# Score pairs three ahead and one behind the projection products in the last sections of a fused Fourier-mixing and attention kernel

## The chip, the cores and the metric

The kernel runs on one core of a Trainium2 chip. The metric is the device time of one execution in microseconds (us), lower is better; the median of the runs shown is taken.

## The reference

Two branches of the same input x (2048 tokens of 512 numbers) are mixed by a gate:

```python
g = _sigmoid((x * gate_w).sum(-1, keepdims=True))
# a: Fourier mixing, real part only
a1 = einsum("bsd,ed->bse", x, dft_hid_re);  b1 = einsum("bsd,ed->bse", x, dft_hid_im)
a  = einsum("ts,bse->bte", dft_seq_re, a1) - einsum("ts,bse->bte", dft_seq_im, b1)
# b: softmax attention, 32 heads of 16, scale 16 ** -0.5
q, k, v = split_heads(x @ wqkv)
b  = merge_heads(softmax(q @ k.T * scale) @ v) @ wo
return g * a + (1 - g) * b
```

(The names are shortened; wqkv and wo are scaled so that the scores are large.)

## The kernel before

**Attention in units.** The 32 heads are taken as 16 pairs. The scores of a pair are computed transposed: 128 keys on the partitions, 512 queries along the row. A unit is one pair, 128 keys and 1024 queries, which makes 512 units (`UNITS`). A unit needs four score tiles of 128x512, one for each of two heads and two blocks of queries. `scores` (L782) issues the matmul of one such tile (L795, PE) and its exponential (L796, ACT), which goes from PSUM to the SBUF tile `pt`. The operands of a score matmul lie on 64 partitions: head 0 on partitions 0 to 63, head 1 on 64 to 127. The matmuls of the two heads therefore run side by side in the two halves of the array, and the two together are called a pair of score matmuls here. `values`, through `pv` (L843) and for the last 16 units through `pv_last` (L803), multiplies the exponentials with the values and accumulates in the bank `acc`; four narrow products run side by side, so that the 16 matmuls of two calls show as one group.

**PSUM.** There are eight banks. Bank 6 is `acc`, one bank belongs to the pool `psD` (tiles named d), and the other six form two rings of three: `psS` (tiles named s) and `psA` (tiles named a). `Ring.tile` (L51) takes the bank of its ring that was used longest ago, where a use is the allocation of a tile or, by `finish` (L659), the reading of a finished product. A matmul that takes a bank waits until the last reader of the tile before has ended.

**The last sections.** Most of the kernel is a stream of short patterns in which Fourier products and projection products alternate with scores. The change is behind them, in the loop over `u` from 492 to 510 in steps of two (L1044): ten sections of two units each. A section issues four pairs of score matmuls (`i` = 0 to 3; head 0 goes to an s bank, head 1 to an a bank, from the list `three`), then two calls of `values`, which take the two units of the section before. Between the pairs stand the section's whole projection products: matmuls over all 128 partitions (L469), listed in `whole` as (generator, number of matmuls). A generator yields chains of nine or three matmuls into one bank, and behind the last matmul of a chain `finish` puts the result on DVE (L668). The first chain of a section goes to an s bank in section 492, to the bank d in 494 to 506, and to an a bank in 508 and 510; in 496, 498, 500 and 504 a second chain goes to an s bank. The chains of 508 are a, d, s, and those of 510 are a, d, s, a. In section 506 `turn` (L728) and in 508 `back` (L739) of the object `LastPair` are issued behind the products: `turn` sums and transposes the first half of the last head pair's output into an s bank, from which DVE makes `on` (L734, L736); `back` transposes `on` into an a bank, which ACT and DVE read (L102, L103). Just ahead of section 492 stand four single score matmuls of head 1, in the banks s, s, a, d (L1034).

Each engine works through its own queue in the written order: the schedule is written by hand (`manual_schedule`), and nothing reorders it.

Of the kernel before, what the change touches and what calls it, by code (L numbers as in the profile page):

```python
# [31 lines left out]
def mix_kernel(ctx: ExitStack, tc: tile.TileContext, xa_t, xa, wqkv, w_hid, w_seq, wo, gate_w, out):  # L32
# [749 lines left out]
    def scores(u, qb, h, bank=(psS, "s"), number=None):  # L782
        p, r = divmod(u, 32)
        hf, kt = divmod(r, 16)
        q0 = hf * 1024 + qb * 512
        if u >= UNITS - 16:

            blk, kt = divmod(kt, 8)
            q0, kt = 1024 + blk * 512, 2 * kt + qb
        if u not in pts:  # L790
            pts[u] = work.tile([P, 4, 512], F32, name="pt", bufs=4)
        pool, name = bank
        ps = pool.tile([P, 512], F32, name=name) if number is None else pool.tile([P, 512], F32, name, number)
        rr = slice(64 * h, 64 * h + (64 if p else 50))
        nc.tensor.matmul(ps, ks[p % 2][rr, kt * P:(kt + 1) * P], qs[p % 2][rr, q0:q0 + 512], start=True, stop=True)  # L795
        return nc.scalar.activation(pts[u][:, 2 * qb + h], ps, AF.Exp, bias=0.0, scale=DH ** -0.5)  # L796
# [74 lines left out]
    def pump(gen, n):  # L871
        for x in take(gen, n, False):
            issue(x, None)
# [35 lines left out]
    def run_plan(u):  # L909
        for v in sorted(v for v in plan if v <= u + 1):  # L910
            for f in plan.pop(v):
                f()
# [32 lines left out]
    def values(close=False):  # L945
        nonlocal valued
        i = pv(valued, close)
        valued += 1
        return i
# [94 lines left out]
    for u in range(valued + 2, UNITS, 2):  # L1044
        run_plan(u)
        for i in range(4):
            if i == 2:
                for gen, n in whole[u]:
                    pump(gen, n)
                if u == 506:  # L1050
                    last_pairs[0].turn()
                elif u == 508:
                    last_pairs[0].back()
            for h in range(2):
                scores(u + i // 2, i % 2, h, three[h])
        values()
        values()
# [40 lines left out]
```

## Time and profile before

| what | value |
|---|---|
| time, median of 3 runs | 1666.66 us (1665.65 to 1666.8) |
| profiled execution, its own time | 1666.87 us |
| its span in the profile | 1665.0 us |
| PE (TensorE matmul), busy | 1655.8 us, 13040 matmuls |
| DVE, busy | 1380.5 us |
| ACT, busy | 1266.4 us |
| granted TensorE clock, mean | 0.999 |
| ten last sections (first score pair of 492 to the products behind 510) | from about 1601 to 1651.78 us in the span |

In rows of the timeline the first number is the start in us from the beginning of the span and the second is the length in us; then come the engine, the line, the operation, the tiles it writes and reads, its shape and how often it stands there. A bracket at the end is the idle time of the engine ahead of the row, and what ended it. The lengths of matmuls overlap, because they are pipelined: what a group costs is read from its start to the start of the next group.

### The profile page before, as it was taken

Reading aid. Unit: us, or ns where it says so; the run is one execution under the profiler, and the core shown is the slowest. Engines: PE = TensorE matmul, PEld = TensorE weight load, DVE = VectorE, ACT = ScalarE, POOL = GpSimd, SP = SyncE. Lnnn points to the kernel's source line nnn. Section 1 sums busy time; section 2 is a strip of 40 time slices with the busy share of each in tenths; the row PEclk is TensorE's granted clock in tenths of the full one; section 3 lists DMA queues with packets and bytes.
Section 4 is the critical chain, followed back from the end, with each engine's and each line's share of the span. In section 5 each row is a group of like instructions: output and inputs, shape, how many; then the busy total and the mean of one; then the engine's idle time right before and its main releaser. Section 6 shows DMA issues by size and latency. Waiting matters only on the chain.

```text
span 1665.0 us, 34810 instructions
## 1 busy us (share of the span) xinstructions
PE 1655.8 (99%) x13040; PEld 1008.9 (61%) x13040; DVE 1380.5 (83%) x2361; ACT 1266.4 (76%) x2469; POOL 720.2 (43%) x734
## 2 busy tenths in 40 slices
PE   9999999999999999999999999999999999999998
PEld 7888855556556655666566655665566656644443
DVE  5439888888888888888888888888888888899954
ACT  5312388888888888888888888888788878889996
POOL 0202144454444456544444465554445556433430
PEclk9999999999999999999999999999999999999999
DMA  8973610414151342414157434315141535462114
GB/s 289 349 163 111 185 17 8 70 34 85 40 96 47 70 110 81 97 46 78 46 88 254 88 118 94 88 57 91 51 86 58 111 104 118 141 188 40 34 34 140
DMA packets 82690, 166.71 MB, mean 100 GB/s; under 512 B 19664, under 2 KB 20158, under 8 KB 78510
## 3 DMA queue, kind: packets, MB, share of 16 engines
q1 hardware_dynamic: 78282, 163.53, 39.1%
q8 instruction: 103, 1.69, 0.5%
q0 software_dynamic: 3808, 0.30, 0.2%
q14 instruction: 65, 0.53, 0.1%
q10 hardware_dynamic: 432, 0.66, 0.1%
HBM read 109.14 MB, written 54.65 MB: 98 GB/s over the span
## 4 chain that ended last, share of the span: by engine, by line
PE 98%; DMA 1%; DVE 0%; issue 0%; POOL 0%; ACT 0%; SPq 0%; DVEq 0%; POOLq 0%; ACTq 0%
PE acc L843 28%; PE d L469 24%; PE a L291 18%; PE s L795 16%; PE s L383 3%; PE s L415 1%; PE d L383 1%; PE a L108 1%; PE a L106 1%; PE s L108 1%; PE s L106 1%; PE a L107 1%; PE s L107 1%; PE a L469 1%; PE s L469 0%; DMA raw<-xa_t 0%
## 5 line engine op out<-in xcount | busy, mean ns | idle before, releaser
L293 DVE TENSOR_REDUCE mx<-a 128x1 f32<-128x512 f32 x2026 | 1259.5, 683 | 170.9 <-PE a L291 144.6
L796 ACT ACTIVATE pt<-s 128x512 f32<-128x512 f32 x2006 | 1022.0, 621 | 33.7 <-PE s L795 17.8
L291 PE MATMUL a<-ks,qs 64*128 64x512 f32 (+1 forms) x2026 | 723.8, 407 | 0.0
L795 PE MATMUL s<-qs,ks 64*128 64x512 f32 (+1 forms) x2006 | 664.2, 395 | 0.8 <-DVE on L736 0.6
L469 PE MATMUL d<-xab,ch 64*128 64x512 f32 x2016 | 644.8, 394 | 0.0
L823 POOL TENSOR_TENSOR oe<-oe,part 128x512 f32<-128x512 f32 x215 | 278.4, 1295 | 597.4 <-ACT part L822 594.9
L291 PEld LDWEIGHTS a<-ks,qs 64*128 64x128 f32 (+1 forms) x2026 | 361.2, 184 | 213.7 <-issue 118.2
L843 PE MATMUL acc<-pt,vt 128*17 128x512 f32 (+1 forms) x3968 | 487.2, 599 | 0.0
L795 PEld LDWEIGHTS s<-qs,ks 64*128 64x128 f32 (+1 forms) x2006 | 361.4, 184 | 71.3 <-ACT pt L796 27.3
L469 PE MATMUL d<-xab,cl 64*128 64x512 f32 x1008 | 397.9, 395 | 0.0
L469 PEld LDWEIGHTS d<-xab,ch 64*128 64x128 f32 x2016 | 366.7, 184 | 27.1
L822 ACT COPY part<-acc 128x512 f32<-128x512 f32 x215 | 126.3, 588 | 187.5 <-PE acc L843 186.5
L843 PEld LDWEIGHTS acc<-pt,vt 128*17 128x17 f32 (+1 forms) x3968 | 92.9, 102 | 218.6 <-issue 138.9
L469 PEld LDWEIGHTS d<-xab,cl 64*128 64x128 f32 x1008 | 185.6, 184 | 13.6
L454 POOL TENSOR_TENSOR cl<-craw,ch 128x512 fp32r<-128x512 f32 x126 | 162.4, 1289 | 10.1
L469 PE MATMUL d<-wre,xab 64*128 64x512 f32 x336 | 90.4, 402 | 0.0
L469 PEld LDWEIGHTS d<-wre,xab 64*128 64x128 f32 x336 | 59.9, 184 | 40.3 <-issue 12.1
L453 POOL CAST ch<-craw 128x512 fp32r<-128x512 f32 x126 | 77.1, 612 | 16.2 <-PE s L795 13.6
L323 POOL DMA_DIRECT2D qs<-mt x119 | 67.2, 570 | 9.9 <-PE a L291 4.9
L469 PE MATMUL d<-wo_hl,o_hl 64*128 64x512 f32 (+1 forms) x246 | 65.2, 397 | 0.0
L102 ACT CAST hl<-s 128x512 fp32r<-128x512 f32 x28 | 16.2, 588 | 58.9 <-PE s L383 31.3
L469 PEld LDWEIGHTS d<-wo_hl,o_hl 64*128 64x128 f32 (+1 forms) x246 | 44.2, 185 | 16.4 <-ACT pt L796 10.2
(172 smaller groups left out, 1034.0 us busy)
## 6 DMA issues: line engine op xcount, KB each, us to landing
craw<-w_seq SPq DMA_DIRECT2D x128, 256.0 KB
qk<-hl SPq DMA_DIRECT2D x32, 512.0 KB
qs<-qk SPq DMA_DIRECT2D x96, 128.0 KB
ks<-qk SPq DMA_DIRECT2D x96, 128.0 KB
b<-hl SPq DMA_DIRECT2D x16, 512.0 KB
xab<-b SPq DMA_DIRECT2D x16, 512.0 KB
o<-oe SPq DMA_DIRECT2D x62, 128.0 KB
oh<-nh SPq DMA_DIRECT2D x12, 512.0 KB
```

The lines of the kernel that those rows point to most:

```text
L291: nc.tensor.matmul(ps, qs[p % 2][r, qt * P:(qt + 1) * P], ks[p % 2][r, kb * 512:(kb + 1) * 512], start=True, stop=True)
L293: user = nc.vector.tensor_reduce(mx[p % 2][:, h, qt, kb:kb + 1], ps, AX.X, ALU.max)
L323: (nc.gpsimd if own else nc.sync).dma_start(rows.rearrange("v (q b c) -> v b q c", q=8, b=4)[:, b], mt[hf][32 * b + h:32 * b + 32:2])
L383: i = nc.tensor.matmul(ps, st[r], mv[r], start=not half and not j, stop=half == 1 and j == 11)
L453: nc.gpsimd.tensor_copy(h1, raw)
L454: nc.gpsimd.tensor_tensor(l1, raw, h1.bitcast(F32), ALU.subtract)
L469: i = nc.tensor.matmul(self.ps, st[r], mv[r], start=not self.begun, stop=stop)
L795: nc.tensor.matmul(ps, ks[p % 2][rr, kt * P:(kt + 1) * P], qs[p % 2][rr, q0:q0 + 512], start=True, stop=True)
L796: return nc.scalar.activation(pts[u][:, 2 * qb + h], ps, AF.Exp, bias=0.0, scale=DH ** -0.5)
L822: nc.scalar.copy(part[0], acc)
L823: nc.gpsimd.tensor_tensor(total, total, part[0], ALU.add)
L843: i = nc.tensor.matmul(acc[32 * j:32 * j + width], v[:, 16 * h:16 * h + width], pt[:, j], start=begin, stop=done or close)
```

## The change

In the ten sections the place at which the projection products (and `turn` or `back`) are issued moves from behind the second pair of score matmuls to behind the third. The exponentials move with their pairs, so that on ACT the cast of `back` (L102) comes behind six exponentials of section 508 instead of four. The number of instructions on each engine is the same, and the orders on DVE, POOL and SP are unchanged. As the rings hand out banks in the order of use, the chains and pairs of these sections also land on other banks.

```diff
@@ -1044,7 +1044,7 @@
     for u in range(valued + 2, UNITS, 2):
         run_plan(u)
         for i in range(4):
-            if i == 2:
+            if i == 3:
                 for gen, n in whole[u]:
                     pump(gen, n)
                 if u == 506:
```

## The prediction

> **What bounds the kernel now.** I read the page first, then the timeline of PE over the last sections, and beside it that of ACT.
>
> ```profile
> PE 1655.8 (99%) x13040; PEld 1008.9 (61%) x13040; DVE 1380.5 (83%) x2361; ACT 1266.4 (76%) x2469; POOL 720.2 (43%) x734
> PE 98%; DMA 1%; DVE 0%; issue 0%; POOL 0%; ACT 0%; SPq 0%; DVEq 0%; POOLq 0%; ACTq 0%
> ```
>
> The first line is the busy time of the engines, the second the chain that ended last, by engine. PE is busy for 99% of the span and makes 98% of the chain. An edit to PE's order therefore pays only through time that PE loses or stops losing. Section 494 shows what an undisturbed section costs on PE:
>
> ```profile
> 1606.43 0.49 PE L795 MATMUL s<-qs,ks 64*128 64x512 f32 x1
> ...
> 1606.77 0.39 PE L795 MATMUL s<-qs,ks 64*128 64x512 f32 x1
> ...
> 1607.09 1.67 PE L469 MATMUL d<-wo_hl,o_hl 128*128 128x512 f32 x6
> 1608.69 0.50 PE L795 MATMUL s<-qs,ks 64*128 64x512 f32 x1
> ...
> 1609.03 0.39 PE L795 MATMUL s<-qs,ks 64*128 64x512 f32 x1
> ...
> 1609.36 1.91 PE L843 MATMUL acc<-pt,vt 128*17 128x512 f32 x16
> 1611.20 0.50 PE L795 MATMUL s<-qs,ks 64*128 64x512 f32 x1
> ```
>
> From start to start: the two leading pairs take 0.34 and 0.32 us, the six products 1.60 (so a chain of three takes 0.80), the two pairs behind 0.34 and 0.33, and the values 1.84. Nothing idles. The same stretch on ACT, whose exponentials free the score banks:
>
> ```profile
> 1607.02 0.60 ACT L796 ACTIVATE pt<-s 128x512 f32<-128x512 f32 x1 [0.51 <-PE a L795]
> 1607.52 0.59 ACT L796 ACTIVATE pt<-a 128x512 f32<-128x512 f32 x1
> 1607.99 0.60 ACT L796 ACTIVATE pt<-s 128x512 f32<-128x512 f32 x1
> 1608.47 0.62 ACT L796 ACTIVATE pt<-a 128x512 f32<-128x512 f32 x1
> ```
>
> ACT starts 0.59 us behind the first pair, so the s bank of that pair is free 1607.62 - 1606.43 = 1.19 us and its a bank 1608.11 - 1606.43 = 1.68 us behind the pair's start. The next exponentials follow in steps of (1608.47 - 1607.02) / 3 = 0.48. These delays are what the change runs into.
>
> **Part 1: the pairs themselves.** Four pairs stay four pairs, but 2 + 2 becomes 3 + 1. What three in a row cost is shown by three rounds of another row-tiled product behind the last section:
>
> ```profile
> 1651.78 0.49 PE L751 MATMUL s<-w,o 32*128 32x512 f32 x1
> ...
> 1652.12 0.39 PE L751 MATMUL s<-w,o 32*128 32x512 f32 x1
> ...
> 1652.35 0.39 PE L751 MATMUL s<-w,o 32*128 32x512 f32 x1
> ...
> 1652.68 1.91 PE L803 MATMUL acc<-pt,vt 128*17 128x512 f32 x16
> ```
>
> The first costs 0.34, the middle one 0.23, the last 0.33: a round is 0.23, and entering or leaving the row tiling adds about 0.10 each. So three pairs cost 0.90. No row shows a lone pair. If it pays both ends, it costs 0.23 + 0.20 = 0.43; if the ends overlap, no less than 0.33, the price of a pair with one end. From above the nearest row is a single full product, 0.55 us to the next group, part of which is a wait for ACT:
>
> ```profile
> 1654.53 0.50 PE L469 MATMUL s<-wo_hl,o_hl 128*128 128x512 f32 x1
> 1655.08 1.10 PE L732 MATMUL s<-pairsum,oe 128*128 128x64 f32 x8
> ```
>
> I take 0.43, since both ends are in the rows above. Then 0.90 + 0.43 = 1.33 stands against 1.34 before: nothing, ten times. The ends give -0.10 or +0.12 per section, so -1.0 to +1.2 us over ten. [...]
>
> **Part 2: sections whose products open in the bank d (494 to 506).** The third pair takes the third bank of each ring, so the next s chain must use the first pair's s bank again. It starts 0.90 + 0.80 = 1.70 us behind that pair and needs 1.19: no wait. If this cover went (ACT late by over 0.5 us), each 0.1 us beyond would cost 0.1 us in 496, 498, 500 and 504. The fourth pair starts 1.7 us or more behind the first and lands on the first or second pair's banks. Of these the latest is the second pair's s bank, by ACT's 0.48 steps free at about 1.19 + 0.96 = 2.15, wanted at 0.90 + 1.60 = 2.50 where an s chain stands; where none does, the banks are the first pair's, free at 1.19 and 1.68, wanted from 1.70 on: just enough. ACT is no bound: eight exponentials are 8 x 0.48 = 3.8 us in a section of 4.77 (1606.43 to 1611.20), and in a section with three products, shorter by 0.8, still 4.0. The values use exponentials of the section before, which end earlier than now. Cost 0.
>
> **Part 3: section 492.** Its products open in the s ring, behind four extra scores, where ACT is in arrears. First PE, then ACT:
>
> ```profile
> 1601.13 0.50 PE L795 MATMUL s<-qs,ks 64*128 64x512 f32 x1
> ...
> 1601.62 2.35 PE L469 MATMUL s<-wo_hl,o_hl 128*128 128x512 f32 x9
> ...
> 1604.25 0.39 PE L795 MATMUL s<-qs,ks 64*128 64x512 f32 x1
> ...
> 1604.58 1.92 PE L843 MATMUL acc<-pt,vt 128*32 128x512 f32 x16
> ```
>
> ```profile
> 1600.45 1.12 ACT L796 ACTIVATE pt<-s 128x512 f32<-128x512 f32 x2
> 1601.42 0.64 ACT L796 ACTIVATE pt<-a 128x512 f32<-128x512 f32 x1
> ...
> 1602.37 0.67 ACT L796 ACTIVATE pt<-s 128x512 f32<-128x512 f32 x1
> ```
>
> The four extra scores are exponentials one to four; the row at 1602.37 is the first pair's s tile. Now the products use the bank of the second extra score, freed at 1600.45 + 1.12 = 1601.57, and start at 1601.62, so a release takes 0.05. In the changed order the third pair takes that bank, its a tile the bank of the third extra score (1602.06), and the products get the first pair's s bank: 1602.37 + 0.67 + 0.05 = 1603.09. They start 1.47 us later; behind them stands one pair of 0.43 instead of two (1604.58 less 1604.25 is 0.33 for the second, the first 0.34). Net 1.47 - 0.24 = +1.23 us.
>
> **Part 4: section 510.** Its products open in the a ring:
>
> ```profile
> 1645.67 0.49 PE L795 MATMUL s<-qs,ks 64*128 64x512 f32 x1
> ...
> 1646.33 0.97 PE L469 MATMUL a<-wo_hl,o_l 128*128 128x512 f32 x3
> ...
> 1649.28 0.49 PE L795 MATMUL s<-qs,ks 64*128 64x512 f32 x1
> ...
> 1649.94 1.91 PE L803 MATMUL acc<-pt,vt 128*17 128x512 f32 x16
> ```
>
> ```profile
> 1646.75 0.59 ACT L796 ACTIVATE pt<-a 128x512 f32<-128x512 f32 x1
> ```
>
> Now the third a bank is free and the products start at once. In the changed order they need the first pair's a bank: 1646.75 + 0.59 + 0.05 = 1647.39, 1.06 us later than 1646.33. Behind them 0.43 instead of 0.66: net +0.83 us. Then follow the values, the end products and the last pair in one PE queue, with no wait on ACT that was late; the loss reaches the end.
>
> **Part 5: sections 502 and 508, where PE waits now.**
>
> ```profile
> 1625.71 0.50 PE L795 MATMUL s<-qs,ks 64*128 64x512 f32 x1 [0.17 <-DVE yp L668]
> ```
>
> ```profile
> 1637.61 1.91 PE L803 MATMUL acc<-pt,vt 128*17 128x512 f32 x16
> 1640.12 0.47 PE L795 MATMUL s<-qs,ks 64*128 64x512 f32 x1 [0.59 <-DVE on L736]
> ...
> 1640.78 0.96 PE L469 MATMUL a<-wo_hl,o_l 128*128 128x512 f32 x3
> ```
>
> Both first pairs wait for an s bank that DVE still reads: the last s chain of 500, and `turn` of 506. In the changed order the first pair finds a free bank and the second waits, 0.34 later. In 502 that is enough: about -0.2. In 508 the first pair starts at 1637.61 + 1.84 - 0.2 = 1639.25, the second still at 1640.12, and the products, which open in the first pair's a bank, not before 1639.25 + 1.68 + 0.05 = 1640.98. That is 0.20 later than 1640.78, less 0.23 for the pair that no longer stands behind: about 0 for both sections together, the 0.2 being inside it. `back` takes the second pair's a bank, free long before its turn. Its cast waits on ACT behind two more exponentials, with two exponentials instead of four queued behind it; ACT idles there, and only the end products need the cast, eight us on.
>
> [...]
>
> **The sum.** 1.23 + 0.83 + 0 + 0 = +2.06 us. The profiled execution took 1666.87 us for a span of 1665.0, 1.87 outside it, and lies 0.2 above the median of 1666.66. I add 2.1 to the median: **1668.8 us**, +0.13%.
>
> **The rivals.**
>
> *Forecast: bank waits in 492 and 510 alone, about +2.1.* Chance 0.62. With part 1's own bounds +1.1 to +3.3.
>
> *The ends of a lone pair overlap (0.33).* For it: PE starts a group before the last one's modelled end (values at 1609.36, pair ends 1609.42). Against it: every first and last pair pays. It gives -1.0, a little less since in 508 DVE sets the second pair's start: about +1.2, 1667.9 us. Chance 0.15.
>
> *The lone pair drains twice, slower by over 0.2%.* Place: the ten single pairs between products and values. Each enters 64-row tiling and leaves it before the array is full; if the next group waits for the pair's whole end, 0.50 us (1608.69), plus the entry's 0.10, it costs 0.60, 0.17 more than taken, 1.7 in all: +3.8, 1670.5 us. It decides from 0.55 us on, which the single full product reaches but with ACT's wait in it. [...] The rows agree with 0.10 per end in groups of two and more. Chance 0.17.
>
> *The waits are hidden and the change gains.* If PE's early start lets ACT run ahead, so that 492 and 510 lose nothing, what is left is -0.2 in 502, about -0.3 in 508 and up to -1.0 from overlapping ends: -1.5, 1665.2 us. Against it: ACT cannot start before the pair it reads, and 1.68 exceeds 0.90. Chance 0.06. That the change does not do what it says is excluded: the built order on PE has three pairs ahead in all ten sections.
>
> **How the numbers follow.** About 0.2% (3.3 us) is what a measurement of this kernel can tell from no change; the runs shown spread over 1.15 us. Forecast, overlap and gain all end within it: same 0.62 + 0.15 + 0.06, less 0.01 for a gain beyond 0.2% and 0.02 for the forecast's upper end, is 0.80; slower 0.17 + 0.02 = 0.19; faster 0.01. The range runs from the overlap case less half the runs' spread, 1667.3, to the drained pair's 1670.5; what is left out is the gain and the tail above.
>
> **What would show it.** In the profile after: in 492 the nine products start about 1.5 us behind the third pair's s matmul, released by ACT `pt` L796; in 510 the first a chain starts about 1.7 us behind the first pair; 502's wait is gone, in 508 the wait for `on` stands ahead of the second pair; lone pairs at 0.43 us; sections 494 to 500 as long as now to 0.1 us. It is wrong if PE waits in 494 to 506, if the lone pair lies outside 0.33 to 0.55, or if the tail behind 510 changes its length.

## The result

| | before | changed |
|---|---|---|
| time, median of 15 runs | 1666.66 us (1665.3 to 1667.2) | 1669.26 us (1668.42 to 1671.2) |
| profiled execution, its own time | 1666.87 us | 1671.2 us |
| its span | 1665.0 us | 1669.1 us |

The ratio of the times is 1.0018 (95% interval 1.0011 to 1.0024): the change makes the kernel slower by 1.8 to 4.0 us, 2.6 us by the medians. The forecast was 1668.8 us in a range of 1667.3 to 1670.5. The profiled execution of the changed kernel is the slowest of its 15 runs, for a reason that the profile shows.

First the page of the changed kernel, its busy times:

```profile
PE 1660.0 (99%) x13040; PEld 1011.5 (61%) x13040; DVE 1379.8 (83%) x2361; ACT 1265.7 (76%) x2469; POOL 718.8 (43%) x734
```

The work of the other engines is the same to 1.5 us, and PE is busy for 4.2 us more with the same 13040 matmuls. Of this 1.0 us lies in the first 100 us, far ahead of the change (98.50 against 97.51 us busy), and 2.3 us in section 492, where single matmuls fill the time and, as shown below, the products take longer. The list of waits of PE between 1600 and 1656 us (who waits for whom, us in total, times, longest) shows the waits, the first two lines for before, the last two for the changed kernel:

```profile
PE s L795 <- DVE on L736: 0.6, 1, 0.6
PE s L795 <- DVE yp L668: 0.2, 1, 0.2
```

```profile
PE a L469 <- ACT pt L796: 1.2, 2, 0.8
PE s L469 <- ACT pt L796: 0.5, 1, 0.5
```

Both old waits, for DVE, are off the list, and three waits for ACT stand there, all at the opening of a product group: 492 (s), 508 and 510 (a). The wait for `on` has only become too short for the list: the second pair of 508 starts 0.52 us behind the first (1642.64 and 1643.16) instead of 0.34. The timeline of PE in section 492 of the changed kernel, from the last extra score on:

```profile
1601.30 0.39 PE L795 MATMUL d<-qs,ks 64*128 64x512 f32 x1
...
1602.19 0.50 PE L795 MATMUL s<-qs,ks 64*128 64x512 f32 x1
1602.68 0.50 PE L795 MATMUL a<-qs,ks 64*128 64x512 f32 x1
1603.66 3.91 PE L469 MATMUL s<-wo_hl,o_hl 128*128 128x512 f32 x9 [0.48 <-ACT pt L796]
1607.51 0.49 PE L795 MATMUL s<-qs,ks 64*128 64x512 f32 x1
...
1607.94 1.93 PE L843 MATMUL acc<-pt,vt 128*32 128x512 f32 x16
```

The third pair and the nine products start where the banks come free. The bank of the products is freed by the exponential of the first pair's s tile, which ends at 1603.60:

```profile
1602.93 0.67 ACT L796 ACTIVATE pt<-s 128x512 f32<-128x512 f32 x1
```

But the products then take 1607.51 - 1603.66 = 3.85 us, where 2.29 was their price before. The table by stretches says why. Behind each stretch stand its length, the busy time of PE, PEld, DVE, ACT and POOL, the granted clock of TensorE, and last the share and the rate of the DMA:

```profile
1602.00:1603.00 1.00, 1.00 (x4) 0.37 (x2) 0.00 (x0) 1.00 (x4) 0.92 (x3) 1.00 0.23 66
1603.00:1604.00 1.00, 0.52 (x2) 0.30 (x2) 0.21 (x1) 1.00 (x4) 0.86 (x2) 0.96 0.00 0
1604.00:1605.00 1.00, 1.00 (x4) 0.76 (x3) 0.00 (x0) 1.00 (x4) 1.00 (x1) 0.50 0.03 10
...
1606.00:1607.00 1.00, 1.00 (x3) 0.75 (x3) 0.00 (x0) 0.06 (x1) 0.00 (x0) 0.50 0.03 4
1607.00:1608.00 1.00, 1.00 (x8) 0.25 (x10) 0.39 (x1) 0.00 (x0) 0.00 (x0) 0.83 0.01 2
```

The granted clock falls to 0.50 just behind the start of the products and is back at 1 in 1607.3. A mean of 0.96 means half clock for 0.08 of the first microsecond, 0.83 for 0.34 of the last; with the three full ones between that makes one spell of 3.42 us. What stands ahead of it, from about 1601.7 to 1603.66, is called the thin stretch below: PE runs score matmuls there mostly one by one, each when ACT frees its bank, and then waits for 0.48 us.

Section 510, and the pairs around it, in the changed kernel:

```profile
1647.12 1.91 PE L803 MATMUL acc<-pt,vt 128*17 128x512 f32 x16
1648.96 0.50 PE L795 MATMUL s<-qs,ks 64*128 64x512 f32 x1
...
1649.31 0.40 PE L795 MATMUL s<-qs,ks 64*128 64x512 f32 x1
...
1649.55 0.39 PE L795 MATMUL s<-qs,ks 64*128 64x512 f32 x1
...
1650.70 0.96 PE L469 MATMUL a<-wo_hl,o_l 128*128 128x512 f32 x3 [0.76 <-ACT pt L796]
...
1653.64 0.50 PE L795 MATMUL s<-qs,ks 64*128 64x512 f32 x1
...
1654.07 1.91 PE L803 MATMUL acc<-pt,vt 128*17 128x512 f32 x16
```

The products start 1.74 us behind the first pair, when the exponential of its a tile has ended at 1650.65:

```profile
1650.06 0.59 ACT L796 ACTIVATE pt<-a 128x512 f32<-128x512 f32 x1
```

The lone pair behind them takes 1654.07 - 1653.64 = 0.43 us.

From one landmark to the next, the two profiled executions compare so:

| stretch | before | changed | difference |
|---|---|---|---|
| start to the last extra score (d) | 1600.72 | 1601.30 | +0.58 |
| from there to the values of 492 | 3.86 | 6.64 | +2.78 |
| to the values of 508 | 39.25 | 39.18 | -0.07 |
| to the values of 510 | 6.11 | 6.95 | +0.84 |
| to the end of the span | 15.06 | 15.03 | -0.03 |

The first row lies ahead of the change, where both programs have the same order: it is the spread from one execution to the next. Of the second row 1.56 us are the half clock; the other 1.22 are the later start of the products, less what one pair behind them saves.

### The profile page after: what moved, and what is told of

It is laid out like the page before. It is cut to its first block, busy times and chain, and to the rows that moved or that the text cites. A ratio compares the mean times of both kernels' runs of the same rounds, so it can differ in the third digit from the quotient of the medians.

```text
span 1669.1 us, 34802 instructions
## 1 busy us (share of the span) xinstructions
PE 1660.0 (99%) x13040; PEld 1011.5 (61%) x13040; DVE 1379.8 (83%) x2361; ACT 1265.7 (76%) x2469; POOL 718.8 (43%) x734
## 4 chain that ended last, share of the span: by engine, by line
PE 99%; DMA 0%; ACT 0%; issue 0%; DVE 0%; DVEq 0%; SPq 0%; ACTq 0%
PE acc L843 28%; PE d L469 25%; PE a L291 17%; PE s L795 16%; PE s L383 3%; PE s L415 1%; PE d L383 1%; PE a L108 1%; PE a L106 1%; PE s L108 1%; PE s L106 1%; PE a L107 1%; PE s L107 1%; PE acc L803 1%; PE s L469 1%; PE a L469 1%
## 5 line engine op out<-in xcount | busy, mean ns | idle before, releaser
L102 ACT CAST hl<-s 128x512 fp32r<-128x512 f32 x28 | 16.1, 587 | 58.9 <-PE d L383 16.5
```

## The experiments

Times are medians; the kernel before on the same chip had 1666.54 us beside the first four experiments, 1666.58 beside the four from "The bank without the move" on, and 1666.26 beside the last one and the repeat of the eight sections. Sections are compared in the traces between the same landmarks as above, since no median of one section's edit is clear of its interval.

**Section 492 alone.**

```diff
-            if i == 2:
+            if i == (3 if u == 492 else 2):
```

> Only section 492 has three pairs ahead; the other nine keep two and two. Theory A (bank wait, and behind it sometimes a spell at half clock): the nine products start 1.47 us later than before, when ACT has freed the first pair's s bank; net +1.23 us from the section's first pair to its values at full clock, and up to +2.8 us where the clock falls as in the profile after. Median +1.2 to +2.8. Theory B (the wait alone, the half clock of the one profile was chance): +1.2, no granted clock under 1 in this section. Theory C (the loss comes from the ten lone pairs): about +0.1.

Measured 1667.72 us, ratio 1.0007 (0.9998 to 1.0016): by itself not clear of no change. The trace:

```profile
1600.26 0.39 PE L795 MATMUL d<-qs,ks 64*128 64x512 f32 x1
...
1602.63 2.32 PE L469 MATMUL s<-wo_hl,o_hl 128*128 128x512 f32 x9 [0.49 <-ACT pt L796]
1604.88 0.50 PE L795 MATMUL s<-qs,ks 64*128 64x512 f32 x1
...
1605.32 1.92 PE L843 MATMUL acc<-pt,vt 128*32 128x512 f32 x16
```

The same wait, but the products take 2.25 us: the clock held, at 1.00 in every microsecond from 1600 to 1608. From the last extra score (d) to the values it is 5.06 us, +1.20 against the 3.86 of before. So the wait costs 1.2 us in both traces, and the half clock comes on top in some executions only.

**The changed kernel once more**, unedited.

> The changed kernel once more, unedited, for a second trace of section 492. Theory A: the product start in 492 is again released by ACT 2.6 us behind the first pair; the nine products take either about 2.3 us (clock held) or up to 3.9 us (half clock), and the runs spread over about 1.6 us more than those of the kernel before. Theory B: the products take 2.3 us and the runs lie as close together as before.

Measured 1668.93 us, ratio 1.0016 (1.0007 to 1.0025). Its trace has the same d, and products that start at the same time as in the experiment above:

```profile
1600.27 0.39 PE L795 MATMUL d<-qs,ks 64*128 64x512 f32 x1
...
1602.63 3.90 PE L469 MATMUL s<-wo_hl,o_hl 128*128 128x512 f32 x9 [0.49 <-ACT pt L796]
1606.47 0.50 PE L795 MATMUL s<-qs,ks 64*128 64x512 f32 x1
```

```profile
1602.00:1603.00 1.00, 0.51 (x2) 0.37 (x2) 0.21 (x1) 1.00 (x4) 0.59 (x1) 0.82 0.00 0
...
1606.00:1607.00 1.00, 1.00 (x8) 0.40 (x11) 0.42 (x1) 0.00 (x0) 0.00 (x0) 0.98 0.01 2
```

Up to the products the two executions agree to 0.01 us, and one falls to half clock and the other does not. Nothing in the order of PE up to there tells them apart. The spell lasts 0.36 + 3 + 0.04 = 3.40 us. The mean granted clock of a whole run shows the spell too, though coarsely. It is rounded to 0.001, which is what a spell costs (half of 3.4 us in 1669), and in the traces before and after the change the clock also falls at the end of the kernel (at 1662.78 and 1665.37 us), behind the last matmul. So 0.998 marks a run with a spell, and 0.999 does not exclude one. Of the 26 runs of the changed kernel seven have 0.998, and their medians are 1670.4 and 1670.2 us in the two sets, against 1669.1 and 1668.9 for the others; single runs of the two groups overlap.

**Section 510 alone.** The same edit with 510 in place of 492.

> Only section 510 has three pairs ahead. Theory A: the first a chain waits 0.76 to 0.82 us for ACT, net +0.83 us, and no spell at half clock, because PE is dense until 0.8 us before. Theory C (lone pairs): +0.1. Rival D: the wait is too long for the clock here too, and the twelve products run slow: +2 or more.

Measured 1667.41 us, ratio 1.0006 (0.9997 to 1.0015).

```profile
1645.98 0.50 PE L795 MATMUL s<-qs,ks 64*128 64x512 f32 x1
...
1647.71 0.96 PE L469 MATMUL a<-wo_hl,o_l 128*128 128x512 f32 x3 [0.77 <-ACT pt L796]
...
1651.09 1.91 PE L803 MATMUL acc<-pt,vt 128*17 128x512 f32 x16
```

From the first pair to the values it is 5.11 us against 4.27 before: +0.84, at full clock: the twelve products take 2.94 us (2.95 before), the mean clock of this execution is 1.000, and no run of ten has one under 0.999.

**The eight sections between.**

```diff
-            if i == 2:
+            if i == (2 if u in (492, 510) else 3):
```

> Three pairs ahead in the eight sections 494 to 508, two and two in 492 and 510. Theory A: no bank wait but the one in 508, which replaces the wait for on; the time from the first pair of 494 to the values of 508 is 0 to 0.1 us below before, the median the same within 0.5 us. Theory C: eight lone pairs, +0.8 to +1.4.

Measured 1665.93 us, ratio 0.9997 (0.9988 to 1.0006). The trace, at the two places where it differs from before:

```profile
1605.92 0.50 PE L795 MATMUL s<-qs,ks 64*128 64x512 f32 x1
...
1638.75 0.50 PE L795 MATMUL s<-qs,ks 64*128 64x512 f32 x1
...
1639.57 0.47 PE L795 MATMUL s<-qs,ks 64*128 64x512 f32 x1 [0.32 <-DVE on L736]
...
1640.42 0.96 PE L469 MATMUL a<-wo_hl,o_l 128*128 128x512 f32 x3
...
1643.24 1.91 PE L803 MATMUL acc<-pt,vt 128*17 128x512 f32 x16
```

From the first pair of 494 to the values of 508 it is 37.32 us, against 37.40 before. The time of 508 hangs on when `on` is ready, so the stretch ahead of it tells more: from the first pair of 494 to the values of 506 it is 30.99 against 31.18, shorter by the wait of 502 that is gone. The lone pairs cost nothing. As the median lay 0.6 us under before, more than the trace explains, it was run once more.

> The kernel with three and one in 494 to 508 alone, once more, to see whether its median of 0.6 us under the kernel before is repeated. The traces give 0.1 us for the sections themselves; if the rest was the chip's spread, the difference is now 0 to 0.3 us.

Measured 1666.37 us, ratio 0.9999 (0.9991 to 1.0008): the 0.6 us is not repeated.

**The bank without the move.** The kernel before, with the a ring turned by one bank ahead of the products of 510:

```diff
             if i == 2:
+                if u == 510:
+                    psA.touch(min(psA.banks, key=used.index))
```

> The kernel before with its two and two pairs everywhere; only the a ring is turned by one ahead of the products of 510, so that the first chain gets the first pair's bank, though no pair has moved. Theory A (the bank is the cost): the products start about 1.7 us behind the first pair instead of 0.66, and the section is 1.06 us longer, with no lone pair anywhere. Rival (the position of the pairs is the cost): 510 as before, within 0.1.

Measured 1667.57 us, ratio 1.0007 (0.9998 to 1.0016).

```profile
1644.99 0.50 PE L795 MATMUL s<-qs,ks 64*128 64x512 f32 x1
...
1646.73 0.96 PE L469 MATMUL a<-wo_hl,o_l 128*128 128x512 f32 x3 [1.00 <-ACT pt L796]
...
1650.33 1.91 PE L803 MATMUL acc<-pt,vt 128*17 128x512 f32 x16
```

5.34 us against 4.27: +1.07, and the products start 1.74 us behind the first pair just as in the change. No pair has moved here. The bank is the cost, not the place of the third pair; the change's 0.84 is this wait less what one pair behind the products saves.

**The move without the bank.** The changed kernel, with the chains of 508 and 510 opening in d:

```diff
-    last = proj(0, (3,), three[1:] + three[:1], range(7))
+    last = proj(0, (3,), three[2:] + three[:2], range(7))
```

> The changed kernel, but the chains of 508 and 510 go to d, s, a (and d) instead of a, d, s (and a), so that their first chain needs no ring bank. Theory A: no wait for pt ahead of the products of 508 and 510; 510 from its first pair to its values as long as before (4.27 us, against 5.11 in the change), 508 0.2 to 0.4 shorter; the loss of 492 stays. Median about 1.1 us under the changed kernel. Rival (lone pairs or the later cast are the cost in 510): 510 stays above 5 us.

Measured 1668.05 us, ratio 1.001 (1.0001 to 1.0019), 0.9 to 1.2 us under the two medians of the changed kernel. From its first pair to its values 510 goes from 1647.58 to 1651.87, 4.29 us, with three pairs ahead and one behind: the loss there is gone, which settles the cause in 510 from both sides. Section 492 keeps its wait of 0.48 us, and in this execution its nine products take 3.84 us (1601.92 to 1605.76), as those of the changed kernel do at half clock (3.85); its mean clock is 0.998. 508 did not become shorter:

```profile
1642.27 0.47 PE L795 MATMUL s<-qs,ks 64*128 64x512 f32 x1 [0.92 <-DVE on L736]
...
1642.93 0.96 PE L469 MATMUL d<-wo_hl,o_l 128*128 128x512 f32 x3
```

The wait for ACT is away, but the second pair waits 0.92 us for `on`, whose chain of transfers ended late in this execution (in the other traces this wait goes from too short for the list to 1.02 us, whatever the edit).

**Dense work in the thin stretch.** The changed kernel, with the values of 492 ahead of its products:

```diff
             if i == 3:
+                if u == 492:
+                    values()
+                    values()
```

(and not behind them).

> The changed kernel, but in 492 the two calls of values stand ahead of the products and behind the third pair, so that dense matmuls fill the wait for the first pair's bank. Theory A with the half clock set off by the thin stretch ahead of the products: no granted clock under 1 in 492, products 2.3 us in every profile, and the section (first pair of 492 to first pair of 494) 0.3 to 0.5 us over before instead of 1.2 to 2.8; the runs lie as close together as those of before, median 1.2 to 1.7 under the changed kernel. Rival (the half clock comes from the program's phase or the long run before, not from the thin stretch): it shows in some runs still.

Measured 1669.24 us, ratio 1.0017 (1.0008 to 1.0026). The half of it about the clock came as expected: the products take 2.27 us at a granted clock of 1.00, and no run of eleven has a mean under 0.999. The half about the time did not:

```profile
1605.70 0.49 PE L795 MATMUL s<-qs,ks 64*128 64x512 f32 x1
...
1606.61 0.49 PE L795 MATMUL s<-qs,ks 64*128 64x512 f32 x1 [0.18 <-DVE yp_qs L668]
...
1607.37 0.50 PE L795 MATMUL a<-qs,ks 64*128 64x512 f32 x1
1607.79 1.65 PE L469 MATMUL d<-wo_hl,o_hl 128*128 128x512 f32 x6
1609.38 0.50 PE L795 MATMUL s<-qs,ks 64*128 64x512 f32 x1
...
1609.81 0.62 PE L843 MATMUL acc<-pt,vt 128*17 128x512 f32 x4
```

The last pair of 492 now stands next to the three of 494, four pairs in a row over three banks. The third pair of 494 needs, for its a tile, the bank that the last pair of 492 filled at 1605.70, and gets it at 1607.37. The wait went from 492 into 494: from d (1599.77) to the values of 494 it is 10.04 us against 8.64 before, +1.40, and the gain expected from 492 is spent.

**A longer thin stretch.** The kernel before, with all four pairs of 492 ahead of its products.

```diff
-            if i == 2:
-                for gen, n in whole[u]:
+            if i == (3 if u == 492 else 2):
+                for gen, n in whole[u] if u != 492 else ():
...
+        if u == 492:
+            for gen, n in whole[u]:
+                pump(gen, n)
         values()
```

> Kernel before, but in 492 all four pairs stand ahead of the products and none behind: the thin stretch, in which PE runs only single score matmuls as ACT frees banks, is about 1 us longer than in the change. Theory A: products start about 4.1 us behind the section's d score's end of the page before, 2.5 us later than before; at full clock the section is +1.8 us. If the thin stretch sets off the half clock, it does so in more runs than in the change (7 of 26 runs of the change lie in the upper group), and the granted clock falls in most. Rival (chance, or a fixed place in time): no more often.

Measured 1670.14 us, ratio 1.002 (1.001 to 1.0029). The products start 3.34 us behind d (1603.67 less 1600.33), 2.44 us later than before, and from d to the values it is 7.10 us.

```profile
1604.00:1605.00 1.00, 1.00 (x4) 0.79 (x3) 0.00 (x0) 1.00 (x4) 1.00 (x1) 0.57 0.01 2
...
1607.00:1608.00 1.00, 1.00 (x10) 0.26 (x12) 0.46 (x1) 0.00 (x0) 0.00 (x0) 0.73 0.03 4
```

Here the spell lasts 0.86 + 2 + 0.54 = 3.40 us. Six of nine runs have a mean clock of 0.997 or 0.998 and lie at 1669.39 to 1671.43; the other three lie at 1667.77 to 1668.59. Counted over all sets, a mean of 0.998 or less stands for four pairs ahead in 492 in 6 of 9 runs, for three ahead in 10 of 47, for two ahead or with the values in between in 0 of 64, and for the kernel before in 0 of 86. A wait alone does not bring it: the two kernels that wait 0.77 and 1.00 us in 510, behind dense work, and have two pairs ahead in 492 are 20 of the 64. The spell belongs to the thin stretch in 492, and grows more frequent with its length.

**What the runs point to.** Two and two in 492, three and one from 494 on, chains of 508 and 510 from d.

> The best that the runs so far point to: two and two in 492, three and one in the nine sections from 494 on, and the chains of 508 and 510 opening in d instead of an a bank. Theory A: no wait for pt ahead of any product group, no half clock; 492 as before, 510 at 4.27 us, 508 shorter by what the first pair does ahead of the wait for on (0.3 us or less). Median 0.2 to 0.6 us under the kernel before. Rival: the gain of 508 goes into the wait for on, which a chain of transfers ends; the same as before within 0.2 us.

Measured 1666.06 us, ratio 0.9998 (0.9989 to 1.0007): not to be told from the kernel before. The 0.20 us under it lie at the edge of both cases of the expectation. The trace speaks for the rival: 510 takes 4.27 us, no product group waits for `pt`, and the second pair of 508 waits 0.59 us for `on`, as the first pair did before. No version found beats the kernel before beyond the measurement.

## Why the prediction was right

*The sum.* Forecast +2.06, measured +2.6 by the medians, within the range. By the landmarks the sections lose 1.22 - 0.07 + 0.84 - 0.03 = 1.96 us at full clock: the likeliest case, bank waits in 492 and 510 alone, carried it. The prediction held about 3.3 us for the least that a measurement of this kernel can tell from no change; with 15 runs of each kernel 2.6 us are told from no change too (1.0011 to 1.0024).

*Part 1, the lone pair.* Taken at 0.43 between ends of 0.33 and 0.55; the trace has 0.43 (1653.64 to 1654.07). Three pairs in a row step by 0.34, 0.24 and 0.32 where nothing waits (494 in the changed kernel), 0.90 as forecast. Both rivals on the pair, overlap and double drain, fall: they would make the sections 494 to 508 shorter by 0.8 or longer by 1.4, and they are 0.08 shorter. That a lone pair leaves the tiling before the array is full, as the second of them supposed, no run shows; the trace has 0.43 in place of its 0.60.

*Part 3, section 492.* The products were to start 2.37 us behind the extra d score (1603.09 less 1600.72); they start 2.36 behind it (1603.66 less 1601.30). Net +1.23 forecast, 1.20 and 1.22 measured. What the part left out is the clock: it costed the nine products at 2.29 us, as if a wait of half a microsecond could not change the price of what follows.

*Part 4, section 510.* +0.83 forecast, +0.84 measured in two kernels; the cause is shown by taking the bank without the move (+1.07, forecast of the wait alone 1.06) and the move without the bank (4.29 against 4.27).

*Part 5, 502 and 508.* The wait of 502 is gone, as forecast. In 508 the products start 1.68 us behind the first pair, when its a bank is free; 1.73 was forecast. That the two sections come out at about 0, and the stretch at -0.07, is in part luck. In the five traces with three pairs ahead and the chains opening in an a bank, 508 takes 6.31 to 6.33 us from the values of 506 to its own, whenever `on` is ready. In the five with two pairs ahead it takes 5.91 to 6.64, in step with a wait for `on` of 0.29 to 1.02. The forecast compared with the wait of one execution, 0.59. This wait is set by transfers and not by PE: ahead of `on`, DVE makes `o_l` from a product of POOL, and for that product POOL waits 16.3 us for a DMA in the trace before.

*The rest.* 2.6 less 1.96 leaves 0.6 us. The half clock, in at least 7 of 26 runs at about 1.3 us each, lifts the mean by some 0.35, the median by less. And the time outside the span is 2.10 us in the changed kernel (median) against 1.87 in the profiled execution before, and 2.13 against 1.88 in the second set: +0.2 us that the forecast took as unchanged. It shows in the three kernels that have three pairs ahead in all ten sections (2.08 to 2.13), and in none that leaves 492 or 510 alone (1.79 to 1.89); why, no run shows. What is left beyond this is no larger than what single runs differ by.

## What to carry to other kernels

Before an operation is moved ahead of another in a ring of banks, count the banks between them: with a ring of three the third group in a row takes the spare one, and what follows waits for the whole evacuation of the first (here 1.7 us against 0.9 us of matmuls). Only the groups that open in that ring lose; those that open elsewhere hide it, so read each section's opening bank instead of pricing the loop once. In 492 a wait of 0.48 us on TensorE behind thin work was followed, in some executions, by 3.4 us at half clock, which made nine products 1.56 us longer; so time the matmuls behind a new wait at both clocks.

## What the runs showed of the hardware

The granted clock fell to half in 492 in three profiled executions, for 3.42 us (changed kernel), 3.40 (the same once more) and 3.40 (four pairs ahead), though PE's longest gap there was 0.5 us. In a fourth, with the chains of 508 and 510 from d, the nine products take 3.84 us, which points to the same. What preceded it were 2 to 3 us in which 64-row score matmuls ran mostly one by one as ACT freed banks. Longer gaps behind dense work did not make the products behind them slower: 1.00 us in 510 with the bank taken without the move (twelve products in 2.94 us, 2.95 before), and 1.01 us in 508 with four pairs ahead in 492 (nine products in 2.19 us, 2.18 before).

The fall does not follow from the kernel's own order alone. With 492 alone and in the changed kernel once more the products start at 1602.63, behind the same wait of 0.49 us; in the first the clock stays at 1.00, in the second it falls at 1602.64. Nor does it fall at a fixed distance from the products (times in the span; the first from stretches of 0.2 us, the others from stretches of 1 us):

| execution | products of 492 start | clock falls | behind the start |
|---|---|---|---|
| changed kernel | 1603.66 | 1603.93 | 0.27 |
| changed kernel once more | 1602.63 | 1602.64 | 0.01 |
| four pairs ahead in 492 | 1603.67 | 1604.14 | 0.47 |

At the end of the kernel the distance differs too: the clock falls 2.53 us behind the start of the last matmul in the changed kernel (1665.37 less 1662.84) and 4.07 us behind it in the kernel before (1662.78 less 1658.71). What sets the moment, no run shows.
